# Three edits in an attention and mixture-of-experts kernel: the order of one PSUM copy and two exponentials, a weight decode in two parts, two constant casts moved

## The chip, the cores and the metric

One NeuronCore of a Trainium2 chip runs the whole program. The metric is device microseconds of one execution. Engines: TensorE (PE, with its weight loads PEld), VectorE (DVE), ScalarE (ACT), GpSimd (POOL), SyncE (SP), which here issues the DMAs.

## What is computed

Causal attention with a decay, on 4 x 8 heads of 576 tokens and width 64, then a dense gated layer, then a routed layer with 8 experts. Only the first part is touched by the change, apart from weights of the second that are prepared during it.

```python
scores = scale * np.matmul(q, k.transpose(0, 1, 3, 2))
decay = cum[:, :, :, None] - cum[:, :, None, :]
scores = np.where(causal, -1000000000.0, scores + decay)
scores = scores - np.max(scores, axis=-1, keepdims=True)
attn = np.exp(scores)
attn = attn / (np.sum(attn, axis=-1, keepdims=True) + 1e-09)
out = np.matmul(attn, v)
...
x = (silu(x @ w_gate) * (x @ w_val)) @ w_out
...
```

## The kernel before

Attention goes over 16 pairs of heads (`run`, L235). While pair p's probabilities are transposed and multiplied with the values, the scores of pair p+1 are made, so one turn of the loop holds both. The 576 queries are five tiles (0 to 4, tile 4 with all 576 keys).

`qk(p, i)` (L119) makes the scores of tile i for both heads: PE products into PSUM tiles `ps_s` (L144; tile 4 in two halves of 288 keys), DVE reductions that add the mask, take the row extreme and write the scores to SBUF (L151), and two ACT exponentials that sum their rows (L158). `tr(p, g)` (L161) transposes the probabilities in four groups, g = 0 to 3, into PSUM tiles `ps_t`, of which there are two; PE instructions are L170, L185, L187 and L180, the copies out of PSUM are ACT's L172 (group 0) and L193 (first head), and DVE's L191 (second head; both heads in group 3). The text calls group 2 the third and group 3 the fourth. Group 3's transposes write the two `ps_t` tiles that the copies of group 2 release. `av(p, g)` (L196, products L201) multiplies a group with the values. `rb` (L204) and `rt` (L210) make the reciprocals of the row sums, transpose them on PE (L214, once in a pair, just after group 0) and spread them by DMA (L219, L221). `xout` (L223) copies the result out of PSUM (L228 ACT, L229 DVE) and scales and splits it on POOL (L230, L232, L233).

In turn p, PE's order is that of the program: group 0, L214, scores of tiles 2 and 3; group 1, `av` 0, tile 4; group 2, `av` 1, tiles 1 and 0; group 3, `av` 2, `av` 3. PE alone is in written order (`manual_schedule`). The other engines' queues are put in order by a planner that takes the traced order as priority and simulates when each instruction becomes ready; `with issue_after(x)` adds an edge so that what the block traces on x's engine is queued behind x.

`run` calls two hooks of `tile_kernel`: `early` (L891) at the start of a turn, `late` (L899) after group 1's copies. At p = 1, `early` calls `cst.rest()` (L861): the DMA of constants (L863) and two DVE casts (L864, L865) of `U` and `ones`, which only the routing after the dense layer uses. From p = 2, every even turn fetches one part of the dense layer's first weights (L304), and every odd turn (3 to 13) decodes it.

The decode (L307) turns 64-bit floats into fp32 pairs: ACT's Square (L314), three DVE integer instructions L315, L316, L317 that build the word from both halves, POOL's L320 and L321 (test for tiny values), L326 (high part) and L329 (low part). In `late` it is queued behind group 1's ACT and DVE copies:

```python
with tc.issue_after(at.mark[0].ins), tc.issue_after(at.mark[1].ins):
    m1.decode(*todo.pop(0), eng=nc.gpsimd)
```

`mark[0]` and `mark[1]` are the last ACT and DVE copies that `tr` traced.

Of the kernel before, what the change touches and what calls it, by code (L numbers as in the profile page):

```python
# [13 lines left out]
ACTF = mybir.ActivationFunctionType  # L14
# [25 lines left out]
class Attention:  # L40
# [64 lines left out]
    def load(self, p):  # L105
        nc = self.nc
        qk = self.R[p] = self.raw.tile([128, 2, S], F32, name="qk")
        nc.sync.dma_start(out=qk, in_=self.io["qk"][2 * p:2 * p + 2].rearrange("a d t s -> (a d) t s"))
# [7 lines left out]
        ins = self.nc.sync.dma_start(out=self.dk[p % 2][61:67], in_=self.cd[2 * p:2 * p + 2].rearrange("a r s -> (a r) s"))  # L116
        self.mark[2] = self.mark[2] or ins

    def qk(self, p, i):  # L119
        nc = self.nc  # L120
        r, d = self.R[p], self.dk[p % 2]
        q0, m = QT[i]
        w = q0 + m
        rs = self.rs[p % 2]
        if p not in self.E:
            self.E[p] = [self.ep.tile([128, 1536], F32, name="e") for _ in range(2)]
        es = ([self.e0[2 * (p % 2) + a] for a in range(2)] if i == 0 else
              [e[:, EO[i]:EO[i] + w] for e in self.E[p]])
        mask = self.cst["mask"]
        off = 448 + m - w if m == 128 else 512  # L130
        b = 128 - m
        prev = [None, None]
        for lo, hi in [(0, w)] if w <= 512 else [(0, w // 2), (w // 2, w)]:
            n = hi - lo
            ps = [self.ps_s.tile([128, 512], F32, name="ps_s") for _ in range(2)]
            for c in range(2):
                for a in range(2):
                    h = 64 * a
                    x, y = r[h:h + 64, 0, q0:w], r[h:h + 64, 1, lo:hi]
                    if c and p:  # L140
                        x, y = self.neg[h:h + 64, :m], d[h:h + 64, lo:hi]
                    elif c:
                        x, y = self.cst["sel"][h:h + 64, :m], self.c8[h:h + 64, lo:hi]
                    nc.tensor.matmul(ps[a][b:, :n], x, y, start=c == 0, stop=c == 1, tile_position=(h, b))  # L144
            for a in range(2):
                mx = self.sm.tile([128, 1], F32, name="mx")
                o, x, y = es[a][b:, lo:hi], ps[a][b:, :n], mask[b:, off + lo:off + hi]
                if i in (1, 2):
                    o, x, y = (t.rearrange("p (b k) -> p b k", k=64) for t in (o, x, y))
                    o = o[:, ::-1]  # L150
                nc.vector.tensor_tensor_reduce(  # L151
                    out=o, in0=x, in1=y, scale=-0.125,
                    scalar=BIGF if prev[a] is None else prev[a][b:], op0=ALU.add, op1=ALU.min, accum_out=mx[b:],
                )
                prev[a] = mx
        for a in range(2):
            c = a * 5 + i
            nc.scalar.activation(es[a][b:, :w], es[a][b:, :w], ACTF.Exp, bias=prev[a][b:], scale=-1.0,  # L158
                                 accum_out=rs[b:, c:c + 1])

    def tr(self, p, g):  # L161
        nc = self.nc
# [72 lines left out]
    def run(self, extra, pool):  # L235
        dec = self.decay_load(pool)
        self.load(0)
        self.cst.load()
        self.decay(*dec)
        self.vload(0)  # L240
        self.load(1)
        self.rows(1)
        with self.tc.issue_after(self.mark[2].ins):
            self.vload(1)
        with self.tc.manual_schedule(engines={PE}):
            self.warm(WARM0)
            for i in (2, 3, 4, 1, 0):
                self.qk(0, i)
            for p in range(NP):
                with self.tc.issue_after(self.mark[2].ins):  # L250
                    if p + 2 < NP:
                        self.load(p + 2)
                    extra[0](p)
                nx = p + 1 < NP
                self.rb(p)
                for g, qs in enumerate(((2, 3), (4,), (1, 0), ())):
                    self.tr(p, g)
                    if g == 0:
                        self.rt(p)
                    elif g == 1:  # L260
                        extra[1](p)
                    if 0 < g < 3:
                        self.av(p, g - 1)
                    if nx:
                        for i in qs:
                            self.qk(p + 1, i)
                for g in range(2, 4):
                    self.av(p, g)
                if p + 2 < NP:
                    self.rows(p + 2)  # L270
                    self.vload(p + 2)
                self.xout(p)
# [14 lines left out]
class MoE1:  # L287
# [19 lines left out]
    def decode(self, r, hi, lo, eng=None):  # L307
        nc = self.nc
        rv = r.rearrange("p (n t) -> p n t", t=2)
        hv, lv = rv[:, :, 1], rv[:, :, 0]  # L310
        t = self.tmp.tile([128, 512], I32, name="dt")
        s = self.tmp.tile([128, 512], F32, name="ds")
        hf = r.bitcast(F32).rearrange("p (n t) -> p n t", t=2)[:, :, 1]
        nc.scalar.activation(s, hf, ACTF.Square)  # L314
        nc.vector.tensor_scalar(t, hv, 0x07ffffff, 3, op0=ALU.bitwise_and, op1=ALU.logical_shift_left)  # L315
        nc.vector.scalar_tensor_tensor(t, hv, -0x40000000, t, op0=ALU.bitwise_and, op1=ALU.bitwise_or)  # L316
        nc.vector.scalar_tensor_tensor(t, lv, 29, t, op0=ALU.logical_shift_right, op1=ALU.bitwise_or)  # L317
        tf = t.bitcast(F32)
        if eng:
            eng.tensor_scalar(s, s, 2.0 ** -30, None, op0=ALU.is_ge)  # L320
            eng.tensor_mul(s, s, tf)  # L321
        else:
            nc.vector.scalar_tensor_tensor(s, s, 2.0 ** -30, tf, op0=ALU.is_ge, op1=ALU.mult)
        s3 = s.rearrange("p (a b) -> p a b", a=hi.shape[1])
        if eng:
            eng.tensor_copy(hi, s3)  # L326
        else:
            nc.scalar.activation(hi, s3, ACTF.Copy)  # L328
        nc.gpsimd.tensor_sub(lo, s3, hi.bitcast(F32))  # L329

    def load(self, g):
        for src, hi, lo in self.parts(g):
            self.decode(self.fetch(src), hi, lo)

    def parts(self, g):
        io = self.io
# [66 lines left out]
H0, WARM0 = 2, 10  # L403
# [435 lines left out]
class Consts(dict):  # L839
# [21 lines left out]
    def rest(self):  # L861
        nc = self.nc
        nc.sync.dma_start(out=self.t[:, 128:], in_=self.src[:, 128:NCST])  # L863
        nc.vector.tensor_copy(self["U"], self.uf[0])  # L864
        nc.vector.tensor_copy(self["ones"], self.uf[1])  # L865


def tile_kernel(tc, io, out, dbg=None):
    nc = tc.nc
    with ExitStack() as ctx:  # L870
# [4 lines left out]
        cst = Consts(nc, cp, io["cst"])  # L875
        wts = Weights(nc)
        wts.pools.append(pool(ctx, "wA", 6))
        with ExitStack() as c1:
# [5 lines left out]
            m1 = MoE1(tc, c1, cst, io, wts, raw, tmp, xth, xtl)  # L884
            with ExitStack() as ca:
                cst.attention(pool(ca, "acst"))
                at = Attention(tc, ca, cst, io, xth, xtl)

                todo = []

                def early(p):  # L891
                    if p == 1:
                        cst.rest()
                    if p == H0:
                        todo.extend(m1.parts(0))
                    if p >= H0 and (p - H0) % 2 == 0 and todo:
                        todo[0] = m1.fetch(todo[0][0]), *todo[0][1:]

                def late(p):  # L899
                    if p > H0 and (p - H0) % 2 and todo:  # L900
                        with tc.issue_after(at.mark[0].ins), tc.issue_after(at.mark[1].ins):
                            m1.decode(*todo.pop(0), eng=nc.gpsimd)

                at.run((early, late), wts.pools[0])
            m1.open(c1)
            wab = [wts.pools[0], pool(c1, "wB", 6)]
            slp = pool(c1, "slots", space=PSUM)
# [6 lines left out]
            for i in range(len(steps) + 1):  # L914
                for f in range(2):
                    if i < len(steps):
                        g, t0, n = steps[i]
# [104 lines left out]
```

## Time and profile before

| what | us |
|---|---|
| median of 3 runs | 1012.9 |
| lowest, highest | 1008.58, 1015.99 |
| the profiled execution, its own time | 1005.57 |
| its span, first to last instruction | 1003.8 |
| PE busy | 944.4 (94%) |
| DVE, ACT, POOL busy | 597.3, 411.9, 228.4 |

The rows below are from that one profiled execution; times in them count from the start of its span. A row of instructions in order of time has the start, the length, engine, line, operation, names, shapes, the number of instructions merged into it, and in brackets how long the engine was idle before it and what ended that.

### The profile page before, as it was taken

The page shows a single profiled execution, that of the slowest core. Times are in us where ns is not written, and L with a number is a line of the kernel's source. Part 1 is how long each engine was busy: PE and PEld are TensorE (multiplying, and loading weights), DVE is VectorE, ACT ScalarE, POOL GpSimd, SP SyncE. Part 2 cuts the span into 40 slices and gives each one's busy share as a digit, 9 for nine tenths or more (in the row PEclk, how much of TensorE's full clock was granted, in tenths as well). Part 3 has the DMA queues.
Part 4 walks back from the last instruction along what each step waited for, and adds up shares of the span by engine and source line. Part 5 has one row for each costly group of instructions (what it writes and reads, how often), then busy time and mean ns, then how long its engine had stood idle before and what let it go on. Part 6 is the DMA issues. An engine that isn't in the chain of part 4 may idle for free.

```text
span 1003.8 us, 16493 instructions
## 1 busy us (share of the span) xinstructions
PE 944.4 (94%) x6282; PEld 847.5 (84%) x6282; DVE 597.3 (60%) x1421; ACT 411.9 (41%) x903; POOL 228.4 (23%) x205
## 2 busy tenths in 40 slices
PE   8899999999999999999999999999899999699893
PEld 5555555579999999999999999998799999699692
DVE  6566776759457468468467455677865554343720
ACT  5556666644343132132132123333554555244620
POOL 1244444442021011011011000000244434631111
PEclk9999999999999999999999999999899999989997
DMA  5344444313122012012012000113576576750400
GB/s 165 102 130 114 143 134 136 107 43 105 43 64 63 1 53 74 1 47 81 1 42 64 1 1 22 43 58 133 185 226 185 183 229 184 231 174 27 132 30 25
DMA packets 53088, 94.83 MB, mean 94 GB/s; under 512 B 5954, under 2 KB 27086, under 8 KB 53007
## 3 DMA queue, kind: packets, MB, share of 16 engines
q1 hardware_dynamic: 47503, 79.58, 26.0%
q0 software_dynamic: 5504, 14.17, 4.2%
q8 instruction: 50, 0.82, 0.3%
q14 instruction: 31, 0.25, 0.1%
HBM read 84.10 MB, written 10.16 MB: 94 GB/s over the span
## 4 chain that ended last, share of the span: by engine, by line
PE 57%; issue 16%; DVE 12%; POOL 6%; ACT 3%; DMA 3%; POOLq 0%; SPq 0%; DVEq 0%; ACTq 0%
PE ps_g L365 23%; PE ps_y L383 12%; PE ps_s L144 4%; DVE dt L316 3%; PE avy L201 3%; PE ps_t L185 3%; PE m_psg L659 3%; PE m_psy L674 2%; PE avx L201 2%; POOL out L700 2%; DVE dt L317 1%; ACT e L158 1%; POOL w L329 1%; DVE e L151 1%; DVE dt L315 1%
## 5 line engine op out<-in xcount | busy, mean ns | idle before, releaser
L365 PE MATMUL ps_g<-xth,w 128*128 128x384 f32 (+1 forms) x1184 | 308.6, 331 | 0.0
L365 PEld LDWEIGHTS ps_g<-xth,w 128*128 128x128 f32 x1184 | 213.1, 188 | 0.6
L365 PE MATMUL ps_g<-xtl,w 128*128 128x384 f32 (+1 forms) x592 | 196.1, 331 | 0.0
L383 PE MATMUL ps_y<-hh,w 128*128 128x384 f32 (+1 forms) x592 | 161.2, 333 | 2.9 <-DVE y L389 2.2
L659 PE MATMUL m_psg<-ygh,w 128*128 128x304 f32 x512 | 117.4, 311 | 1.2 <-ACT b_o L809 0.8
L674 PE MATMUL m_psy<-h2h,w 128*128 128x304 f32 x512 | 114.6, 306 | 0.5 <-issue 0.5
L383 PEld LDWEIGHTS ps_y<-hh,w 128*128 128x128 f32 x592 | 107.1, 188 | 5.8 <-DVE y L389 4.0
L329 POOL TENSOR_TENSOR w<-ds,w 128x512 fp32r<-128x512 f32 x36 | 49.8, 1384 | 271.9 <-ACT w L328 271.4
L365 PEld LDWEIGHTS ps_g<-xtl,w 128*128 128x128 f32 x592 | 111.2, 188 | 0.1
L158 ACT ACTIVATE e<-e,mx 128x320 f32<-128x320 f32 (+4 forms) x160 | 88.5, 555 | 51.7 <-DVE mx L151 51.2
L586 DVE TENSOR_TENSOR w<-raw,w 128x1024 fp32r<-128x1024 f32 x64 | 76.8, 1222 | 37.9 <-ACT w L585 22.4
L383 PE MATMUL ps_y<-hl,w 128*128 128x384 f32 (+1 forms) x296 | 97.9, 331 | 0.5 <-DVE hl L373 0.5
L372 ACT ACTIVATE hh<-hs 128x384 fp32r<-128x384 f32 (+1 forms) x74 | 38.2, 517 | 134.4 <-DVE hs L371 134.4
L370 DVE SCALAR_TENSOR_TENSOR hs<-hs,ps_g 128x384 f32<-128x384 f32 (+1 forms) x74 | 40.0, 541 | 86.4 <-ACT hs L369 86.4
L659 PEld LDWEIGHTS m_psg<-ygh,w 128*128 128x128 f32 x512 | 87.4, 193 | 1.8 <-ACT b_o L809 0.9
L674 PEld LDWEIGHTS m_psy<-h2h,w 128*128 128x128 f32 x512 | 85.5, 188 | 0.3
L151 DVE CUSTOM_DVE_ANT_0 e<-ps_s,mask 128x320 f32<-128x320 f32 (+4 forms) x160 | 62.6, 429 | 37.5 <-PE ps_s L144 36.6
L585 ACT ACTIVATE w<-raw 128x1024 fp32r<-128x1024 f32 x64 | 67.5, 1059 | 34.1 <-PE m_psg L659 13.3
L659 PE MATMUL m_psg<-ygl,w 128*128 128x304 f32 x256 | 78.4, 306 | 0.5 <-DVE ygl L627 0.5
L389 DVE TENSOR_TENSOR y<-ps_y,y 128x384 f32<-128x384 f32 (+1 forms) x124 | 67.2, 542 | 19.0 <-PE ps_y L383 18.2
L369 ACT ACTIVATE hs<-ps_g 128x384 f32<-128x384 f32 (+1 forms) x74 | 35.4, 479 | 104.6 <-PE ps_g L365 104.5
L674 PE MATMUL m_psy<-h2l,w 128*128 128x304 f32 x256 | 77.4, 302 | 0.0
(305 smaller groups left out, 1520.0 us busy)
## 6 DMA issues: line engine op xcount, KB each, us to landing
raw<-w SPq DMA_DIRECT2D x64, 512.0 KB
qk<-qk SPq DMA_DIRECT2D x16, 576.0 KB
v<-vL SPq DMA_DIRECT2D x16, 448.0 KB
raw<-mg SPq DMA_DIRECT2D x12, 512.0 KB
raw<-mv SPq DMA_DIRECT2D x12, 512.0 KB
raw<-mo SPq DMA_DIRECT2D x12, 512.0 KB
rb<-rd SPq DMA_DIRECT2D x16, 288.0 KB
yd<-yr SPq DMA_DIRECT2D x18, 256.0 KB
```

The costliest lines, as they stand in the source:

```text
L144: nc.tensor.matmul(ps[a][b:, :n], x, y, start=c == 0, stop=c == 1, tile_position=(h, b))
L151: nc.vector.tensor_tensor_reduce(out=o, in0=x, in1=y, scale=-0.125, scalar=BIGF if prev[a] is None else prev[a][b:], op0=ALU.add, op1=ALU. ...
L158: nc.scalar.activation(es[a][b:, :w], es[a][b:, :w], ACTF.Exp, bias=prev[a][b:], scale=-1.0, accum_out=rs[b:, c:c + 1])
L201: nc.tensor.matmul(self.X[x][64 * a:64 * a + 64, d0:d0 + n], v[k0:k0 + k, a, j], self.T[g, a][k0:k0 + k, o:o + n], start=g == 0, stop=g == ...
L329: nc.gpsimd.tensor_sub(lo, s3, hi.bitcast(F32))
L365: nc.tensor.matmul(ps[:, :n], w[:, k, fs], x[:, k], start=(k == 0 and c == 0), stop=(k == 3 and c == 2))
L383: nc.tensor.matmul(ps[:, :n], w[:, f, ds], h[:, f, :n], start=(f == 0 and c == 0), stop=(f == 1 and c == 2))
L389: nc.vector.tensor_add(y, ps[:, :n], y)
L585: nc.scalar.activation(hi, r, ACTF.Copy)
L586: nc.vector.tensor_sub(lo, r, hi.bitcast(F32))
L659: nc.tensor.matmul(ps[:, :C], w[:, k, fs], x[:, k], start=(k == 0 and c == 0), stop=(k == 3 and c == 2))
L674: nc.tensor.matmul(self.P[e][d][:, :C], w[:, f, ds], h[:, f], start=(u == 0 and f == 0 and c == 0), stop=(u == 3 and f == 1 and c == 2))
```

## The change

Tile 4's two exponentials are no longer traced with its scores but returned as a function, and traced in the next group's step behind group 2's ACT copy (`issue_after(mark[0])`). `decode` becomes a generator with one `yield`: Square and L315 stay in `late`, the rest (L316, L317 and the POOL instructions) is traced in a third hook, `last`, after group 2's copies and queued behind them on ACT and DVE; no edge is added on POOL. The two casts of constants move from turn 1's start to a function `split`, traced in `last` of turn 2; the DMA of the constants stays. Elsewhere the decode runs through both parts at once, as before.

```diff
-    def qk(self, p, i):
+    def qk(self, p, i, later=False):
...
-        for a in range(2):
-            c = a * 5 + i
-            nc.scalar.activation(es[a][b:, :w], es[a][b:, :w], ACTF.Exp, bias=prev[a][b:], scale=-1.0,
-                                 accum_out=rs[b:, c:c + 1])
+        def exps():
+            for a in range(2):
+                c = a * 5 + i
+                nc.scalar.activation(es[a][b:, :w], es[a][b:, :w], ACTF.Exp, bias=prev[a][b:], scale=-1.0,
+                                     accum_out=rs[b:, c:c + 1])
+
+        if later:
+            return exps
+        exps()
...
+                exps = None
                 for g, qs in enumerate(((2, 3), (4,), (1, 0), ())):
                     self.tr(p, g)
                     if g == 0:
                         self.rt(p)
-                    elif g == 1:
-                        extra[1](p)
+                    elif g < 3:
+                        extra[g](p)
+                    if exps:
+                        with self.tc.issue_after(self.mark[0].ins):
+                            exps()
+                        exps = None
                     if 0 < g < 3:
                         self.av(p, g - 1)
                     if nx:
                         for i in qs:
-                            self.qk(p + 1, i)
+                            exps = self.qk(p + 1, i, i == 4)
...
         nc.vector.tensor_scalar(t, hv, 0x07ffffff, 3, op0=ALU.bitwise_and, op1=ALU.logical_shift_left)
+        yield
         nc.vector.scalar_tensor_tensor(t, hv, -0x40000000, t, op0=ALU.bitwise_and, op1=ALU.bitwise_or)
...
         nc.sync.dma_start(out=self.t[:, 128:], in_=self.src[:, 128:NCST])
+
+    def split(self):
+        nc = self.nc
         nc.vector.tensor_copy(self["U"], self.uf[0])
         nc.vector.tensor_copy(self["ones"], self.uf[1])
...
+                dec = []
+
                 def late(p):
                     if p > H0 and (p - H0) % 2 and todo:
+                        dec.append(m1.decode(*todo.pop(0), eng=nc.gpsimd))
                         with tc.issue_after(at.mark[0].ins), tc.issue_after(at.mark[1].ins):
-                            m1.decode(*todo.pop(0), eng=nc.gpsimd)
-
-                at.run((early, late), wts.pools[0])
+                            next(dec[0])
+
+                def last(p):
+                    with tc.issue_after(at.mark[0].ins), tc.issue_after(at.mark[1].ins):
+                        if p == H0:
+                            cst.split()
+                        if dec:
+                            for _ in dec.pop():
+                                pass
+
+                at.run((early, late, last), wts.pools[0])
```

## Rows read from the trace of the kernel before

**Rows 1.** Busy time by stage: start:end, us, each engine's busy us, granted clock, DMA

```profile
0.00:218.00 218.00, 199.69 (x1618) 125.19 (x1619) 145.88 (x530) 135.08 (x409) 84.84 (x85) 0.96 0.42 123
218.00:700.00 482.00, 478.52 (x2832) 467.49 (x2832) 304.78 (x640) 145.23 (x285) 46.13 (x33) 1.00 0.15 46
```

**Rows 2.** Windows: pair 0; decode pairs 11, 13, all six; eight others

```profile
17.14:35.21 18.07, 14.49 (x99) 8.80 (x100) 8.01 (x33) 7.69 (x25) 0.17 (x1) 0.81 0.23 64
...
159.84:174.82 14.98, 13.27 (x101) 8.27 (x100) 10.58 (x34) 8.51 (x27) 8.95 (x8) 0.89 0.56 162
186.33:199.94 13.61, 11.89 (x100) 7.35 (x100) 10.60 (x34) 8.51 (x27) 8.66 (x7) 1.00 0.36 103
sum 84.90, PE 74.90 PEld 46.31 DVE 62.63 ACT 50.95 POOL 51.42; mean PE 12.48 PEld 7.72 DVE 10.44 ACT 8.49 POOL 8.57
...
sum 91.29, PE 91.29 PEld 56.70 DVE 61.33 ACT 64.46 POOL 27.17; mean PE 11.41 PEld 7.09 DVE 7.67 ACT 8.06 POOL 3.40
```

**Rows 3.** Who waited for whom, 0 to 222 us: total, times, longest

```profile
PE ps_t L180 <- ACT ath L193: 7.8, 6, 1.4
```

**Rows 4.** In order of time, pair 11 (L214 at 159.84), with a decode

```profile
163.65 0.42 DVE L315 TENSOR_SCALAR dt<-raw 128x512 int32<-128x512 int32 x1
163.74 1.62 POOL L233 TENSOR_TENSOR xtl<-xt,xth 128x576 fp32r<-128x576 f32 x1
...
164.10 1.80 DVE L316 SCALAR_TENSOR_TENSOR dt<-raw,dt 128x512 int32<-128x512 int32 x1
...
165.44 1.82 POOL L320 TENSOR_SCALAR ds<-ds 128x512 f32<-128x512 f32 x1
...
165.94 0.98 DVE L317 SCALAR_TENSOR_TENSOR dt<-raw,dt 128x512 int32<-128x512 int32 x1
...
166.84 0.45 DVE L151 CUSTOM_DVE_ANT_0 e<-ps_s,mask 128x288 f32<-128x288 f32 x1
...
170.31 0.33 PE L180 MATMUL ps_t<-cst,e 64*128 64x64 f32 x2 [1.35 <-ACT ath L193]
```

**Rows 5.** In order of time, pair 14 (L214 at 199.94), no decode

```profile
205.37 0.27 PE L187 MATMUL ps_t<-cst,e 128*128 128x128 f32 x1
...
205.80 0.78 ACT L158 ACTIVATE e<-e,mx 128x576 f32<-128x576 f32 x1 [1.09 <-DVE mx L151]
...
206.12 0.69 DVE L191 COPY ath<-ps_t 128x512 f32<-128x512 f32 x1
...
207.34 0.58 ACT L193 ACTIVATE ath<-ps_t 128x512 f32<-128x512 f32 x1
...
207.85 0.36 DVE L151 CUSTOM_DVE_ANT_0 e<-ps_s,mask 128x192 f32<-128x192 f32 x1 [1.03 <-PE ps_s L144]
207.96 0.20 PEld L180 LDWEIGHTS ps_t<-cst,e 64*128 64x128 f32 x2
...
208.25 0.46 ACT L158 ACTIVATE e<-e,mx 128x192 f32<-128x192 f32 x1 [0.33 <-DVE mx L151]
...
208.95 0.89 DVE L191 COPY ath<-ps_t 128x320 f32<-128x320 f32 x2
...
209.09 1.45 PE L201 MATMUL avy<-ath,v 128*64 128x256 f32 x12
```

**Rows 6.** In order of time, pair 0 (L214 at 17.14)

```profile
29.63 0.23 DVE L864 CAST uo<-cst 128x128 fp32r<-128x128 f32 x1 [4.60 <-DMA cst<-cst]
...
29.90 0.69 DVE L191 COPY ath<-ps_t 128x512 f32<-128x512 f32 x1
...
30.64 0.27 PE L180 MATMUL ps_t<-cst,e 64*128 64x64 f32 x1 [3.58 <-DVE ath L191]
...
31.71 2.35 PE L201 MATMUL avy<-ath,v 128*64 128x256 f32 x12
```

**Rows 7.** The decode's DVE lines in 0 to 222 us: ns least, median, most

```profile
L315 DVE TENSOR_SCALAR dt<-raw x6: 418/526/1620, 61.7 to 190.1; 128x512 int32<-128x512 int32 x6
...
L316 DVE SCALAR_TENSOR_TENSOR dt<-raw,dt x6: 693/1448/1797, 62.3 to 191.7; 128x512 int32<-128x512 int32 x6
```

More of the change, by code (lines that the diff above doesn't have):

```diff
@@ L332, in load @@
         for src, hi, lo in self.parts(g):
-            self.decode(self.fetch(src), hi, lo)
+            for _ in self.decode(self.fetch(src), hi, lo):
+                pass
     def parts(self, g):
@@ L897, in early @@
                         todo[0] = m1.fetch(todo[0][0]), *todo[0][1:]
+                dec = []
                 def late(p):
                     if p > H0 and (p - H0) % 2 and todo:
+                        dec.append(m1.decode(*todo.pop(0), eng=nc.gpsimd))
                         with tc.issue_after(at.mark[0].ins), tc.issue_after(at.mark[1].ins):
-                            m1.decode(*todo.pop(0), eng=nc.gpsimd)
-                at.run((early, late), wts.pools[0])
+                            next(dec[0])
[5 more added lines that the diff above has]
+                            for _ in dec.pop():
+                                pass
+                at.run((early, late, last), wts.pools[0])
             m1.open(c1)
```

## The prediction

> **What bounds the kernel now.** I read the busy times by stage first, then pair by pair, then who waits for whom, then single pairs in order of time. TensorE (PE) sets the end. From 218 to 700 us it is busy 478.52 of 482.00 us, so whatever the first stage gives up is passed on to the end almost whole [rows 1]. The attention stage before it is different: 199.69 busy of 218.00. I cut that stage at the transpose of the reciprocals (L214), which comes once in each pair of heads. The eight pairs that carry no decode take 91.29 us together, PE busy all of it: 11.41 us a pair is PE's own work, and nothing there can be won without taking work from PE. The six pairs with a decode (3, 5, 7, 9, 11, 13) take 84.90 us, 16.4 more than six of the others. Pair 0 takes 18.07 [rows 2].
>
> Two things make up the excess of a decode pair. One is PE's idle time: in six of them the first transpose of the fourth group (L180) waits for ACT's copy L193, 7.8 us in all [rows 3]. The other is the clock. In pair 11, one of three such, the granted clock is 0.89 of full speed on average, so PE was for a while at 1.2 and not at 2.4 GHz, and it is busy 13.27 us with the work that takes 11.41 elsewhere: 1.9 us a pair. Pair 13 kept 1.00 and took 13.61 [rows 2].
>
> Pair 11 shows the chain [rows 4]. The decode's three DVE instructions stand ahead of the reductions of tile 4. L315 takes 0.42, L316 1.80, L317 0.98. Tile 4's reductions begin only when they are through, at 166.84. After the reductions come two exponentials, then the ACT copy, and PE gets its PSUM buffer at 170.31 after 1.35 idle. In pair 14 that copy also stands behind the exponentials (207.34), but it ends at 207.92 and PE takes L180 at 207.96 without a recorded wait [rows 5].
>
> In pair 0 DVE waits 4.60 us for the constants' DMA with the cast L864; the third group's copy L191 stands behind it and starts at 29.90, and PE's second transpose of the fourth group has stood idle 3.58 when it starts at 30.64. The 12 products that follow take 2.35 us [rows 6] against 1.45 in pair 14 [rows 5].
>
> **The change, part by part.** *Constants.* The two casts leave pair 0's stretch and follow the third group's copies of pair 2. Their transfer, landed by 29.6, is then long done. In pair 2 DVE is idle there for 1.03 us (pair 14 stands for it [rows 5]), and 0.23 [rows 6] for each cast hides under that: cost 0; without the cover it is 0.3. What goes in pair 0 is 3.6 of idle and 2.35 - 1.45 = 0.9 of slow clock: 4.5 us. Late next there would be the loads of pair 1 and 2, which are issued where they were; the DMA of the constants stays in SP's place too. Nothing moves past another transfer on SP's queue: the edit moves the casts and leaves the issue.
>
> *Copy before exponentials.* In pair 14 the last transpose for the copy ends at 205.64 and the exponentials of tile 4 begin at 205.80, after ACT has been idle for 1.09 [rows 5]. The copy (0.58) then runs at about 205.7 to 206.3, the exponentials start some 0.5 later and, at 0.78 a step, end at about 207.95, before the first exponential of tile 1 (208.25). Cost 0 there; if that slack of 0.3 were gone, it is up to 0.58 a pair. Behind the copy on ACT wait the two exponentials, and behind them those of tiles 1 and 0; these feed the next pair's reciprocals. In a decode pair the copy no longer waits for reductions that the decode has delayed: the idle 1.35 before L180 goes.
>
> *Decode in two places.* The Square and L315 stay; L316, L317 and the POOL steps move behind the third group's copies. No instruction or DMA is added. I follow a decode pair from its L214 on. DVE's third-group copy ends at +6.8 as in pair 14 (206.81 - 199.94, less the overlap of about 0.1 with which DVE starts the next). L316 and L317 at 0.69 [rows 7] and 0.69 (a twin of it, bounded by 0.98 [rows 4]) run to +8.2. Tiles 1 and 0 began at +7.9 (207.85); they now start 0.3 to 0.6 late, take the 1.1 that they take to the next copy (208.95), and the two copies of the fourth group (0.89) end at +10.2 to +10.5 instead of +9.9. The last products need them: the 12 products that contain them start at +9.15, and the third of them that reads these copies is due two thirds of 1.45 later, at about +10.1 to +10.3. So PE loses 0 to 0.35; I take 11.6 us for the pair. That holds where L315 takes 0.42.
>
> L315 can take 1.62 [rows 7]. In pair 11 it started 0.09 before POOL's L233, and got through at 0.42; L316 started 0.36 behind it and took 1.80 [rows 4]. The least L316 took is 0.69 [rows 7]. L315 stays where it is, next to L233, so I count three slow and three fast. Slow is 1.2 later, of which the fourth group's copies, ending at about +11.1, pass 0.7 on beyond the fast case: 12.3 us. Half of each gives 3 x 11.6 + 3 x 12.3 = 71.7, a gain of 84.9 - 71.7 = 13.2.
>
> The bounds: below, six pairs at 11.41, a gain of 16.4. Above, L316 and L317 at 1.80 and 0.98 in the new place too (1.4 more) on top of the slow L315: 13.7 a pair, a gain of 2.7. I stay near the first, because in the new place POOL has ended L233 (165.36, that is +5.5) and has only L320, begun at +5.6, before it must wait for L317.
>
> The Trainium skill (SBUF — State Buffer, section "Who interferes with whom") says that VectorE and GpSimd share one pair of SBUF ports, and that a GpSimd instruction and a VectorE one with two SBUF inputs, or in a two-port mode, exclude each other for a whole instruction, the later one blocking fully. The trace agrees for L316 (1.80 beside L233, 0.69 at the least). Held strictly, the rule speaks against the new place: L320, recorded from +5.6 for 1.82 us, would hold L316 until +7.4, 0.6 late in each of six pairs, and the sum would come out 3.6 us poorer than mine. It is the first rival's mildest form.
>
> **The sum.** 13.2 + 4.5 = 17.7 us. The profiled execution took 1005.57 us (span 1003.8 and 1.8 around it): 987.9 on its own terms. The runs shown have a median of 1012.9, 7.3 above that execution; taking the same gain from it gives 995.2.
>
> **Rivals.** *POOL holds the second part as well.* POOL's L320 is the next in its queue after L233, and if it holds L316 and L317 as L233 did (1.80 and 0.98), a fast pair becomes 11.6 + 1.4 = 13.0: gain 84.9 - 78.0 + 4.5 = 11.4, 1001.5 us. For: L317 at 0.98 behind L320's start. Against: POOL's next step (L321) must wait for L317, so only one instruction can be in the way.
>
> *Another wait in pair 0.* If PE, 4.5 us earlier at pair 1, meets a load that isn't there, pair 0's part is lost: 13.2 alone, 999.7. Against: the queries and keys were issued ahead of the constants, whose transfer had landed at 29.6.
>
> *The exponentials bind.* They come 0.58 later in all 15 pairs; if the slack of 0.3 on ACT is spent (an ACT copy that waits for PE), the reciprocals of the next pair come late by up to 0.58: 15 x 0.58 = 8.7 given back, gain 9.0, 1003.9.
>
> *Slower.* The lateness moves to the end of the pair: all three decode steps are held by POOL, the fourth group's copies come after av2 is through, PE idles there and the clock falls to 1.2 GHz, which pair 11 prices at 1.9. Then a pair takes 12.3 + 1.4 + 1.9 = 15.6, six 93.6: 8.7 more than before, less 4.5 from pair 0, 1017.1. It decides against the change from 14.9 us a pair on (14.15 now, plus 4.5 / 6).
>
> *The change doesn't do what it says.* DVE and ACT follow an order that a planner makes; if it puts the pieces where the waits stay, the time stays 1012.9. Against: the edges that the change adds are binding for that order.
>
> **How the numbers follow.** Forecast 0.66, POOL 0.13, pair 0 0.08, exponentials 0.07, slower 0.03, nothing 0.03. A measurement of this kernel tells about 1% from no change, 10 us: below 1002.8 is faster. The forecast nearly whole, six tenths of POOL's case, most of pair 0's case and a third of the exponentials' make 0.82; slower by over 1% needs more than the worst rival, 0.02; 0.16 between. The range: 1005 above, which holds the bound of 2.7 + 4.5 = 7.2 but for a fraction and leaves out the last two rivals. Below, all six at 11.41 gives 16.4 + 4.5 = 20.9, 992.0; and if the runs shown lost the clock in the three other decode pairs too (3 x 1.9 of the 7.3 that they lie above the profiled one), the gain grows to 26.6: 986.3, so I say 985.
>
> **What would show it.** Right: decode pairs at 11.4 to 12.5 us with a granted clock of 1.00; L316 at about 0.7; no wait of L180 for L193; ACT's copy ahead of tile 4's exponentials; pair 0 at about 13.5 us; the casts without idle time. Wrong: a new wait of the last products (L201) for DVE's L191 of over 1 us, L316 near 1.8, a clock of 0.89 in a decode pair, or pairs without decode above 11.6.

## The result and the profile after

The changed kernel's first set of runs has a median of 995.81 us (990.16 to 1006.24, 5 runs) beside 1009.75 (1008.32 to 1015.99, 5 runs) for the kernel before on the same chip: ratio 0.9848 [0.9807, 0.9888]. The forecast was 995.2. Two further sets, taken with the experiments, gave 998.66 beside 1009.41, 0.9923 [0.9892, 0.9955], and 999.14 beside 1006.88, 0.992 [0.9899, 0.994]. So the change gains 7.7 to 13.9 us by medians, about 11. That is faster by over 1% in the first set and inside 1% in the others: the direction held, but the gain is smaller than the forecast 17.7 us. The changed kernel also scatters more (995.15 to 1006.97 in the second set) than the kernel before (1006.56 to 1013.17 there, in 12 runs).

The profile first taken of the changed kernel was its slowest run, so I read the one of the second set (995.15 us, span 993.3). L158 is L159 and L180 is L185 after the change, L191 is L196, L193 is L198, L201 is L206, L233 is L238, L315 is L325, L316 and L317 are L327 and L328, L320 is L331, and rd's and rb's DMAs, L219 and L221, are L224 and L226.

Stretches of the changed kernel: pairs 0, 7, 11, 12 and 14; then three stretches of pairs 12 and 13; the last is a stretch of routing, at the start of the routed experts. A row has the stretch, its length, the busy us of PE, PEld, DVE, ACT and POOL, the clock as a share of 2.4 GHz, the DMA share and GB/s. They answer to [rows 1, 2].

```profile
17.19:30.05 12.86, 12.86 (x99) 7.67 (x100) 7.66 (x31) 7.65 (x25) 0.00 (x0) 0.87 0.31 90
99.76:112.84 13.08, 11.70 (x100) 7.05 (x100) 11.11 (x34) 8.57 (x27) 7.45 (x6) 1.00 0.47 125
148.13:159.65 11.52, 11.52 (x100) 7.06 (x100) 9.19 (x34) 8.58 (x27) 3.08 (x3) 1.00 0.45 119
159.65:171.50 11.85, 11.44 (x102) 7.08 (x100) 8.53 (x31) 8.41 (x27) 7.03 (x7) 1.00 0.72 193
183.09:196.72 13.63, 11.52 (x102) 7.29 (x101) 7.67 (x31) 8.04 (x26) 9.30 (x8) 1.00 0.34 104
...
162.00:169.00 7.00, 7.00 (x69) 4.54 (x69) 5.25 (x23) 5.53 (x18) 2.88 (x3) 1.00 1.01 281
169.00:174.00 5.00, 4.59 (x37) 2.69 (x34) 3.42 (x10) 2.77 (x10) 3.46 (x3) 1.00 0.14 51
174.00:175.60 1.60, 1.60 (x18) 0.98 (x18) 1.60 (x6) 1.60 (x6) 0.00 (x0) 1.00 0.00 0
...
695.18:703.18 8.00, 7.40 (x35) 6.61 (x34) 5.48 (x31) 1.68 (x4) 4.16 (x5) 0.50 0.38 94
```

Pair 0 went from 18.07 [rows 2] to 12.86. Pair 11 went from 14.98 at a clock of 0.89 to 11.52 at 1.00. The six decode pairs sum to 72.97 us (11.65, 12.62, 13.08, 12.51, 11.52, 11.59), where they were 84.90. These are 5.2 and 11.9 us. But pair 14, which has no decode, takes 13.63 and loses 2.1 in one wait, and pair 12 takes 11.85; both had 11.5 before. The attention stage ends at 203.18 instead of 217.85 us, 14.7 earlier. The rest of the span took 790.1 instead of 785.9. Of these 4.2, 1.5 are lost in the dense layer (the first product of the routing, `rt_ps<-yh`, starts at 606.00 instead of 619.16) and 1.8 more at the start of the routed experts (their first product, `m_psg<-ygh`, at 703.68 instead of 715.05). The last row shows TensorE at 1.2 GHz there, where the kernel before had 0.93 of 2.4 GHz in the eight us at the same distance from its attention stage (the row stands further down).

PE's waits in the attention stage (total, times, longest), which answer to [rows 3]:

```profile
PE avy L206 <- DVE ath L196: 3.1, 3, 1.4
PE ps_s L144 <- DMA qk<-qk: 2.3, 2, 2.1
```

The wait of the transpose for ACT's copy, 7.8 us before, is gone from the list. Two others stand there in its place. The decode's three instructions (ns least, median, most), which answer to [rows 7]:

```profile
L325 DVE TENSOR_SCALAR dt<-raw x6: 417/417/424, 56.5 to 175.3; 128x512 int32<-128x512 int32 x6
...
L327 DVE SCALAR_TENSOR_TENSOR dt<-raw,dt x6: 682/920/1497, 59.5 to 178.3; 128x512 int32<-128x512 int32 x6
...
L328 DVE SCALAR_TENSOR_TENSOR dt<-raw,dt x6: 692/836/1778, 60.2 to 179.0; 128x512 int32<-128x512 int32 x6
```

In order of time, a pair that is slow and one that is fast (pair 7, begun at 99.76, and pair 11, begun at 148.13); [rows 4] show pair 11 of before:

```profile
105.01 1.42 POOL L235 TENSOR_TENSOR xt<-xt,rb 128x576 f32<-128x576 f32 x1 [9.59 <-DMA rb<-rd]
...
106.54 1.16 DVE L327 SCALAR_TENSOR_TENSOR dt<-raw,dt 128x512 int32<-128x512 int32 x1
...
107.23 1.73 POOL L238 TENSOR_TENSOR xtl<-xt,xth 128x576 fp32r<-128x576 f32 x1
...
107.74 1.78 DVE L328 SCALAR_TENSOR_TENSOR dt<-raw,dt 128x512 int32<-128x512 int32 x1
...
111.06 1.04 PE L206 MATMUL avy<-ath,v 128*64 128x256 f32 x4 [1.38 <-DVE ath L196]
...
153.93 0.60 ACT L198 ACTIVATE ath<-ps_t 128x512 f32<-128x512 f32 x1 [0.48 <-PE ps_t L192]
...
154.43 0.77 ACT L159 ACTIVATE e<-e,mx 128x576 f32<-128x576 f32 x1
...
154.92 0.68 DVE L327 SCALAR_TENSOR_TENSOR dt<-raw,dt 128x512 int32<-128x512 int32 x1
...
155.63 0.69 DVE L328 SCALAR_TENSOR_TENSOR dt<-raw,dt 128x512 int32<-128x512 int32 x1
...
156.12 0.33 PE L185 MATMUL ps_t<-cst,e 64*128 64x64 f32 x2
...
156.43 1.41 POOL L235 TENSOR_TENSOR xt<-xt,rb 128x576 f32<-128x576 f32 x1 [9.95 <-DVE dt L328]
```

The reader is to see three things. ACT's copy now stands ahead of tile 4's exponentials and L185 waits for nothing. L325 is never held in this profile. And in pair 7 POOL's normalisation of the pair before (L235 to L238) starts 5.25 us after the pair's begin, because it has waited 9.59 us for the broadcast of the reciprocals, rb; it then runs beside L327 and L328, which take 1.16 and 1.78 instead of 0.68 and 0.69. The fourth group's copies end 1.4 us too late for the last products. Pairs 5, 7 and 9 lose so; in the profile of the third set it is pairs 5 to 11, at 12.65 to 12.84 us.

What delays rb is seen on SP's queue. First its waits in 60 to 200 us (total, times, longest), then DMA issues in order of time and PE's wait in pair 14, in the changed kernel:

```profile
SPq L226 <- DMA rd<-rt: 94.0, 12, 11.8
```
```profile
162.17 0.63 SPq L224 DMA_DIRECT2D rd<-rt  x1
174.62 0.51 SPq L226 DMA_DIRECT2D rb<-rd  x1
175.18 0.46 SPq L108 DMA_DIRECT2D qk<-qk  x1
...
185.47 0.81 PE L144 MATMUL ps_s<-qk 64*128 64x320 f32 x4 [2.11 <-DMA qk<-qk]
```

The kernel before: the same wait of SP (60 to 215 us), and four stretches.

```profile
SPq L221 <- DMA rd<-rt: 36.6, 13, 3.4
```
```profile
24.00:27.00 3.00, 3.00 (x29) 1.89 (x28) 1.03 (x6) 2.11 (x5) 0.00 (x0) 1.00 0.16 56
27.00:29.60 2.60, 0.06 (x1) 0.00 (x0) 0.00 (x0) 0.00 (x0) 0.00 (x0) 1.00 0.11 44
...
709.85:717.85 8.00, 6.74 (x47) 5.77 (x46) 6.59 (x28) 4.00 (x7) 4.47 (x5) 0.93 0.52 150
```

SP issues rd (the reciprocals, 5 KB, written to memory), waits until it has landed, and issues rb (their broadcast from there over 128 rows); the next pair's queries and keys stand behind rb in SP's order. From rd's issue to rb's it took 2.1 us in pair 1, 5.7 in pair 5, 10.2 in pair 11, and 12.5 in pair 12 (162.17 to 174.62); before, it was 1.2 to 3.8 in the 16 pairs. I call this the lag.

The three stretches from 162 on show why, with the packets that the trace records. The broadcast issued at 159.15 is 128 packets of 2304 bytes. They move from 160.43 to 168.46, 37 GB/s, never more than three at once, while the other loads beside them bring the share to 1.01. Then for 5 us the share is 0.14, that is 2.2 of 16 engines, and 51 GB/s. No packet of the broadcast is left by then: what moves are the last parts of the queries and keys, the weights and the values, which were issued behind it. rd, issued at 162.17, is ten packets of 512 bytes; eight move by 169, and the last two at 173.7, after those parts. Then nothing moves until rb's next issue. From one issue of rb to the next it takes 12.8 us on average (pair 1 to pair 13), in both kernels. Before, TensorE's own round was 12.6 ((84.90 + 91.29) / 14 [rows 2]), so the lag didn't grow. After, TensorE asks for 11.3 to 11.6, and the transfers don't follow. The Trainium skill (DMA: Bandwidth & Descriptors, section "Rules for kernel authors") says that a DMA whose outermost dimension has c under 16 steps, for example a leading broadcast of c copies, is confined to at most c engines; rb's source is [2, 64, S], and the trace agrees: never more than four packets of rb move at once in any pair, and 2.2 of 16 engines are left with work behind it.

### The profile page after: what moved, and what is told of

It reads as the page before. It is cut to its first block, busy times and chain, and to the rows that moved or that the text cites. A ratio compares the mean times of both kernels' runs of the same rounds, so it can differ in the third digit from the quotient of the medians.

```text
span 1004.4 us, 16481 instructions
## 1 busy us (share of the span) xinstructions
PE 943.2 (94%) x6282; PEld 845.8 (84%) x6282; DVE 597.1 (59%) x1421; ACT 412.3 (41%) x903; POOL 227.1 (23%) x205
## 4 chain that ended last, share of the span: by engine, by line
PE 56%; issue 16%; DVE 9%; DMA 8%; POOL 7%; ACT 3%; SPq 0%; another core or an unknown queue 0%; POOLq 0%; DVEq 0%; ACTq 0%
PE ps_g L377 23%; PE ps_y L395 12%; PE ps_s L144 5%; PE m_psy L686 3%; PE ps_t L190 3%; PE m_psg L671 3%; DMA rd<-rt 2%; DVE dt L327 2%; DMA qk<-qk 2%; PE avx L206 2%; PE avy L206 2%; POOL out L712 2%; POOL w L340 1%; DMA raw<-w 1%; POOL b_r L652 1%
## 5 line engine op out<-in xcount | busy, mean ns | idle before, releaser
L159 ACT ACTIVATE e<-e,mx 128x320 f32<-128x320 f32 (+4 forms) x160 | 88.0, 551 | 32.9 <-DVE mx L151 32.4
L686 PEld LDWEIGHTS m_psy<-h2h,w 128*128 128x128 f32 x512 | 86.7, 191 | 0.3
L597 ACT ACTIVATE w<-raw 128x1024 fp32r<-128x1024 f32 x64 | 67.4, 1058 | 40.1 <-PE m_psg L671 12.5
```

The source lines that it names most:

```text
L597: nc.scalar.activation(hi, r, ACTF.Copy)
L686: nc.tensor.matmul(self.P[e][d][:, :C], w[:, f, ds], h[:, f], start=(u == 0 and f == 0 and c == 0), stop=(u == 3 and f == 1 and c == 2))
```

## The experiments

**The three edits, each alone.** Two theories stood against each other: that each edit gives its own term of the sum, or that a transfer sets a floor that any of them reaches. "Copy alone" and "decode alone" have the casts back at their old place; in "copy alone" and "casts alone" the decode is in one piece (the first hunk); "casts alone" and "decode alone" have the exponentials in line (the second).

```diff
-                            next(dec[0])
+                            for _ in dec.pop():
+                                pass
```
```diff
-                            exps = self.qk(p + 1, i, i == 4)
+                            self.qk(p + 1, i)
```

The changed kernel again: 

> The changed kernel once more, for a second profile. Prediction's steps (P): 17.7 us less, ratio 0.982 to 0.983, decode pairs at 11.5 to 12.5 us to the last, no wait for a load. Rival (D), from the first profile after: the transfers have become the bound. There the reciprocals' broadcast (rb) moved at about 50 GB/s with a DMA share of 0.13 for some 5 us, and SP's round of a pair (rd, rb, qk, raw, dk, v) took about 13 us against 11.4 of TensorE, so that the wait between the issue of rd and that of rb grew from 2 us in pair 1 to 12.7 in pair 12. D expects the same growth here, TensorE waiting for queries and keys in pairs 12 to 14, the first decode pairs near 12 and pair 13 at 14 us or more, and a total gain of 13 to 15 us, ratio 0.985 to 0.987.

Measured 998.66, 0.9923 [0.9892, 0.9955]; its profile is the one above. The lag grew to 12.5 us as D had it. The gain is below both ranges, and it was pair 14 and not pair 13 that took over 13 us.

Copy alone: 

> Only the ACT copy ahead of tile 4's exponentials; decode in one piece, casts where they were. P: TensorE's idle before L180 (1.35 us in a decode pair) goes, the 0.35 before tile 1's scores stays, and the clock with less idle time stays up: decode pairs at 12.2 to 12.5, 74 us for six, 11 less: 0.989. Rival (V): VectorE's copy for the second head still stands behind the delayed reductions and takes ACT's place as the last to come, so L180's second transpose waits instead: decode pairs near 14, gain about 1: 0.999. D, in either case: no more than about 8 us, since SP's round is about 12.8 to 13 us a pair: 0.992.

Measured 1000.6, 0.9919 [0.9895, 0.9944]: the number that D gave, but not by D's floor, as its lag shows below.

Casts alone: 

> Only the two casts of constants moved. P: pair 0 takes 13.0 us in place of 18.1, nothing else changes: 4.5 to 5 us less, 0.995. D: the pairs after it already take 12.8 us on average, which is SP's round, so some of the 5 us is given back as waits for loads: 0.997 to 1.000.

Measured 1001.94, 0.992 [0.9892, 0.9947]: more than either theory gave it.

Decode alone: 

> Only the decode in two parts. P: tile 4's reductions are on time, so the ACT copy behind the exponentials is on time as in the pairs without decode, and this edit alone takes the decode pairs to about 12.0: 13 us less, 0.987; with the copy alone at 0.989 the two edits would not add. Rival: the copy behind the exponentials still makes L180 wait by about 0.5, pairs at 12.5: 0.990. D: as for the copy alone, 8 us at most: 0.992.

Measured 1002.71, 0.9927 [0.9902, 0.9952].

By the medians the single edits gain 8.8, 7.5 and 6.7 us, 23.0 together, and all three at once gain 10.8: they do not add. Some of the waits (total, times, longest) follow, for copy alone, decode alone and casts alone, in this order:

```profile
DVE uo L879 <- DMA cst<-cst: 6.4, 1, 6.4
...
PE ps_s L144 <- DVE mx L151: 3.9, 6, 1.0
```
```profile
DVE uo L879 <- DMA cst<-cst: 4.1, 1, 4.1
...
PE ps_s L144 <- DMA qk<-qk: 3.4, 3, 1.9
```
```profile
PE ps_t L185 <- ACT ath L198: 8.0, 6, 1.4
```

Each mechanism appears where the prediction had it: without the moved casts DVE waits 4.1 to 6.4 us for the constants; without copy and split, L185 waits 8.0 in six. With copy alone the whole decode still delays DVE's reductions, and the scores wait 3.9 us for them.

Copy and split overlap: with either one alone the wait of L185 for ACT's copy is gone. The six decode pairs take 77.6 us with copy alone, 74.1 with decode alone and 73.0 with all three, beside 84.9 before. The floor shows in decode alone: its decode pairs 3 to 11 take 11.88 to 12.29, it meets the queries and keys three times, as the changed kernel does in pair 14, and its lag goes to 12.2 us. In copy alone and casts alone the lag stays below 7 us and no such wait exceeds 0.2, so there the floor is not what they reach.

The profiles do not show where the sum of the medians goes. The attention stage ends 6.7 us earlier with copy alone, 2.1 with casts alone and 5.3 with decode alone, 14.1 together, and 14.7 with all three. In casts alone pair 0 gives 3.8, but the decode pairs take 86.7, three of them at a clock of 0.81 to 0.89; its profiled execution took 1006.29, 4.3 above its median. What the medians lack of 23.0 is open.

**The broadcast in two transfers.** If rb's two engines set the floor, two DMAs of 64 rows each must lift it, for the changed kernel and for the kernel before:

```diff
-        self.mark[2] = nc.sync.dma_start(out=rb, in_=d.unsqueeze(1).to_broadcast([2, 64, S]))
+        for a in range(2):
+            self.mark[2] = nc.sync.dma_start(out=rb[64 * a:64 * a + 64], in_=d[a:a + 1].to_broadcast([64, S]))
```

The change with it: 

> The changed kernel with the broadcast of the reciprocals (rb) issued as two transfers of 64 rows each in place of one of 2 x 64. D (the transfers bound the changed kernel, through rb, which moves at 50 GB/s with a DMA share of 0.13, as if on two of sixteen engines, and holds what is queued behind it): rb now takes under 2 us, the wait between rd's and rb's issue stays below 4 us to the last pair, no wait for queries and keys in pair 14 (2.1 us in the second profile), decode pairs 11.5 to 11.9, attention ends at 197 to 199 us in place of 203.2, and the time is 5 to 8 us below the changed kernel's: 0.975 to 0.986 of the kernel before. Rival (S): SP's order is the bound, since rb waits on its queue for rd's landing and everything of the next pair waits behind it, however wide rb is: lag grows to 10 us as it did, time as the changed kernel's.

Measured 972.75 beside 995.39 for the kernel before on the same chip: 0.9762 [0.9739, 0.9785].

The kernel before with it: 

> The kernel before with rb in two transfers and nothing else. If rb's late landing is what puts POOL's scaling and splitting (L230 to L233) beside the decode's VectorE steps, and what keeps the constants' transfer (9.4 us for 237 KB) behind it: POOL is done by 4 us into a pair, L315 and L316 take 0.42 and 0.70 in all six decode pairs, these take 12.2 us as pair 7 did (73 for six, 11 to 12 us less), and the cast's wait of 4.6 falls below 1: 4 more. 0.984 to 0.989. Rival: the POOL steps are held by something else (the order on POOL, ACT's copy), L316 stays at 1.8 in most pairs: 0.995 to 1.0.

Measured 977.65, 0.9819 [0.9797, 0.984]: somewhat more than expected.

In the change with the wide broadcast, pair 11, the stretch of pair 13 in which rb (issued at 173.50) is the only load that moves, and SP's wait in 60 to 200 us:

```profile
145.79:157.31 11.52, 11.52 (x100) 7.06 (x100) 9.20 (x34) 8.58 (x27) 8.00 (x7) 1.00 0.65 207
174.80:176.40 1.60, 1.60 (x16) 0.83 (x16) 1.57 (x5) 1.60 (x4) 0.80 (x1) 1.00 0.63 187
```
```profile
SPq L227 <- DMA rd<-rt: 27.5, 12, 3.6
```

The 288 KB move in 1.6 us at a share of 0.63, 187 GB/s. All decode pairs take 11.5 to 11.7, PE never waits in them, the lag is at most 3.9 us, and the attention stage ends at 198.2. The floor was the broadcast's. A second rival, that SP's own order binds whatever the width, fell with it. The ratio is 0.016 below the changed kernel's, about 16 us and not the 5 to 8 expected. The attention stage gives 5.0 of them, and the dense layer, in which this kernel loses nothing, another 1.5; the rest is not located, and the chips differ.

The other kernel says more. With this one edit and nothing of the change, the attention stage ends at 202.6, as early as the whole change has it. Its views, in this order: the two stretches of pair 0 that stand above for the kernel before; PE's wait; the decode's second instruction; and POOL and DVE in pair 11, begun at 148.84.

```profile
24.00:27.00 3.00, 3.00 (x30) 2.05 (x28) 2.25 (x12) 1.28 (x4) 0.00 (x0) 1.00 0.30 117
27.00:29.60 2.60, 2.60 (x30) 1.65 (x28) 1.77 (x10) 2.26 (x9) 0.00 (x0) 1.00 0.01 3
```
```profile
PE ps_t L180 <- ACT ath L193: 6.1, 6, 1.0
```
```profile
L317 DVE SCALAR_TENSOR_TENSOR dt<-raw,dt x6: 692/694/694, 58.6 to 176.7; 128x512 int32<-128x512 int32 x6
```
```profile
148.93 1.40 POOL L231 TENSOR_TENSOR xt<-xt,rb 128x576 f32<-128x576 f32 x1 [7.79 <-ACT xt L229]
150.39 0.66 POOL L233 CAST xth<-xt 128x576 fp32r<-128x576 f32 x1
151.13 1.42 POOL L234 TENSOR_TENSOR xtl<-xt,xth 128x576 fp32r<-128x576 f32 x1
...
152.66 0.42 DVE L316 TENSOR_SCALAR dt<-raw 128x512 int32<-128x512 int32 x1
153.11 0.69 DVE L317 SCALAR_TENSOR_TENSOR dt<-raw,dt 128x512 int32<-128x512 int32 x1
153.84 0.69 DVE L318 SCALAR_TENSOR_TENSOR dt<-raw,dt 128x512 int32<-128x512 int32 x1
```

(Its lines are one or two beyond those of before.) In pair 0 of the kernel before, the constants landed late because their transfer stood behind the two-engine broadcast: shares of 0.16 and 0.11 from 24 to 29.6, PE idle in the second stretch. With two DMAs they are there by 26.6 and the casts wait for nothing; the pair takes 14.03, at a clock of 0.79. In a decode pair POOL has rb when the pair's sums are ready, and is through at 152.55, 0.11 before the decode's first DVE instruction. So all three run alone, at 0.42, 0.69 and 0.69, and so they do in all six pairs. A decode pair takes 12.2; the 1.0 that is left is L180's wait for ACT's copy, which the copy ahead of the exponentials removes.

**One edit taken out, with and without the wide broadcast.** Is the split of the decode still worth anything when the copy comes first? Copy and casts with the wide broadcast, the decode in one piece: 

> The changed kernel with rb in two transfers, but with the decode in one piece. If POOL is out of the way, one piece costs 1.8 us of VectorE ahead of tile 4's reductions, with the copy first PE loses under 0.7 us a decode pair: 12.0 each, 2 to 4 us slower than with the split. Rival (the split is what matters): pairs of 12.8 to 13 as in the run with the copy alone, 6 to 8 us slower.

Measured 970.99, 0.9759 [0.9737, 0.9781]: neither expectation, it is as fast as with the split.

Casts and split, no early copy, wide broadcast: 

> The changed kernel with rb in two transfers, but with tile 4's exponentials ahead of the copy as before. P: with the decode split the reductions are on time and the copy behind the exponentials makes no wait, so this equals the version with the copy first, within 2 us. Rival: the copy ahead of the exponentials is worth its 0.5 us in each pair: 3 to 7 us slower than with it.

Measured 979.05, 0.9828 [0.9803, 0.9853], 6.3 us slower than with the copy first: the rival's range. Its profile shows a granted clock of 0.95 in every pair after the first, so its stages can't be compared with the others', and it was measured again in the last set: 

> Again the changed kernel with rb in two transfers and the exponentials ahead of the copy. Its first profile had a granted clock of 0.95 throughout, and pairs without decode of 11.6 us. If that was the run's and not the version's: 11.4 for those, 11.9 for the decode pairs (VectorE's order has a reduction between L327 and L328 there), 0.979, some 3 us slower than with the copy first. If it is the version's: 0.95 and 0.983 again.

Measured 991.18, 0.9849 [0.9813, 0.9884], with pairs without decode back at 11.39 us (11.6 in the run before): the 0.95 was of that run, not of the edit. The ratio is again that of the rival all the same. The attention stage ends at 199.3, 1.1 later than with the copy first, so most of the 6 us lies outside it and is not located.

In the same set, the changed kernel: 

> The changed kernel beside the two below on one chip. D: 10 to 16 us less than the kernel before (0.984 to 0.990); the wait between rd's and rb's issue grows past 9 us again and TensorE waits for queries and keys in one of pairs 12 to 14.

Measured 999.14, 0.992 [0.9899, 0.994]: less than expected. The lag grew to 11.9 us, and TensorE waited 0.5 us for queries and keys.

The decode in one piece, rb as it was: 

> Copy first and casts moved, decode in one piece, rb in one transfer as in the changed kernel. P (terms add): 11 for the copy and 5 for the casts less, 16 us, so the split is worth 2 to 3 us of the forecast: 0.984. D: the transfers' round bounds it as it bounds the changed kernel, and the split is worth nothing: within 0.3% of the changed kernel.

Measured 992.7, 0.9861 [0.9838, 0.9884], its four runs within 0.9 us: between the two expectations.

The decode in one piece, wide broadcast: 

> The same with rb in two transfers, the fastest so far, beside the changed kernel: D: decode pairs 11.3 us as all others, 0.976 of the kernel before again, 9 to 15 us below the changed kernel.

Measured 985.75, 0.9788 [0.9756, 0.9819].

With the wide broadcast the split is worth nothing that these runs can tell: 0.9759 without it and 0.9762 with it. Its decode pairs take 11.32 without the split and 11.52 with it (the first 11.66 in both); with the split but no early copy they take 11.87 to 12.03, where PE waits 0.2 a pair for the fourth group's copies:

```profile
PE avy L206 <- DVE ath L196: 1.3, 6, 0.3
```

With rb as it was, the kernel without the split is measured faster than the changed kernel (992.7 and 999.14, intervals apart), though POOL then holds the one-piece decode at its old place. Its decode instructions, and its worst pair:

```profile
L325 DVE TENSOR_SCALAR dt<-raw x6: 417/1099/1536, 55.4 to 179.7; 128x512 int32<-128x512 int32 x6
...
L327 DVE SCALAR_TENSOR_TENSOR dt<-raw,dt x6: 693/1032/1034, 56.0 to 180.2; 128x512 int32<-128x512 int32 x6
...
L328 DVE SCALAR_TENSOR_TENSOR dt<-raw,dt x6: 692/1776/1786, 57.1 to 180.9; 128x512 int32<-128x512 int32 x6
```
```profile
100.66:115.88 15.22, 13.66 (x100) 8.29 (x100) 11.78 (x34) 8.60 (x27) 8.85 (x7) 0.89 0.46 130
```

Its attention stage ends at 205.1 us, 2.6 later than that of the changed kernel in the same set (202.5), whose profiled execution took 990.6, 8.5 below its median. So why the medians stand the other way round is not shown by these profiles. What differs is the lag, 11.9 us in the changed kernel and 8.0 without the split, and with it the dense layer, in which the first loses 1.7 us against the kernel before and the second 0.8.

The best version is the decode in one piece, copy first, casts moved, and the broadcast in two DMAs: 0.9759 and 0.9788 in its two sets, ahead of both kernels. Its interval overlaps that of the version with the split.

## Why the prediction was right, and where it wasn't

*Constants, 4.5 us.* Right: pair 0 gave 5.2, the casts stand in pair 2 without idle time (pair 2 takes 11.32, as pair 1, so no load was late there either). The 3.6 of idle went in every version with the casts moved. The other part, the clock, is not the edit's to give: these versions took 11.32 us in pair 0 at a clock of 1.00 up to 14.25 at 0.78 (casts alone), so the size was partly luck.

*Copy first, cost 0, and the idle 1.35 goes.* Right. The wait went from 7.8 us to none, though the split alone removes it too, and pairs that carry no decode stay at 11.3 to 11.4 but for 12 and 14. The rival in which the exponentials bind fell: it asked 0.58 in each of 15 pairs.

*Decode pairs, 71.7 us.* Measured 72.97, close for a partly wrong reason. The step "I count three slow and three fast" put the slow case on L315 staying beside L233. L325 took 0.42 in all six, so the slow case of 12.3, with its +11.1 that no row gives, was not met. It was the second part that was held, in pairs 5, 7 and 9, which took 12.62, 13.08 and 12.51. This is the rival in which POOL holds the second part, near its price of 13.0, in three of six; the other three took 11.5 to 11.65, the forecast's 11.6. The argument against it, that POOL has ended L233 by then and only L320 can be in the way, took POOL's times of before as given, while they hang on when rb lands, and rb moves later from pair to pair. What ran beside L327 and L328 in these pairs was mostly the normalisation, L235 to L238, which ends with the old L233. L320 (L331) did not hold L327 in pair 3: L327 took 0.68 from 59.48 on, while L331 is recorded from 58.30 to 59.80. In pairs 11 and 13 POOL comes so late that it falls behind the decode altogether (L235 at 156.43). The Trainium skill (SBUF — State Buffer, section "Who interferes with whom") says that a DVE instruction with two SBUF inputs contends with a GpSimd instruction that reads SBUF, and the trace agrees for L235 to L238: L327 takes 0.68 alone and up to 1.50 beside them, L328 0.69 and up to 1.78.

*What is late next.* This step failed. It named the loads of pairs 1 and 2, and said that nothing moves past another transfer on SP's queue. That is so for the order of issue, but nothing asked how long one round of that queue takes. The next limit was rd, rb and the queries and keys behind them, 12.8 us a round against TensorE's 11.4. The lag needs ten pairs to grow, so it costs TensorE a load only in pair 14, where it loses 2.2 us, 2.1 of them in the wait for queries and keys. Pair 12 loses 0.4 by another road: POOL scales so late that DVE's addition ahead of the reciprocals (L212) runs beside it and takes 1.14 us instead of 0.17, and L219 waits for that. The rows read before had the sign: pair 0 and the decode pairs were long in part for one common cause, since the wide broadcast alone removes the constants' wait, the slow decode instructions and the low clock of the decode pairs. It leaves 6.1 of the 7.8 us of L180's wait and a clock of 0.79 in pair 0. Two of the prediction's own signs of being wrong came: the last products wait up to 1.4 us for DVE's copy, and pairs 12 and 14 are above 11.6.

*Passed on to the end almost whole.* This failed too: where the prediction counted 17.7, the attention stage gave up 14.7 in the profile (17.1 in the terms that the sum held, 5.2 + 11.9, less about 2.6 for pairs 12 and 14), and 10.5 of these reached the end. The row it rested on ends at 700 us and shows TensorE busy; what lies behind 700 had no row. The dense layer lost 1.5 and 1.7 us in the two profiles of the changed kernel read here and 1.9 in decode alone, while in the six with the wide broadcast it is within 0.3 of the kernel before. So this loss goes with the broadcast; by which load is not shown. The routed experts are another matter: one profile of the changed kernel loses 2.7 us there, the other gains 1.3, so the change does not explain it.

*The median.* The first set's 995.81 lies on the forecast, partly by luck: the forecast started from 1012.9, the median of three runs, and with two more of the kernel before the start is 1009.75, so the gain was 13.9 and not 17.7. The second and the third set, 0.9923 and 0.992, lie above it, and a gain of 17.7 from 1009.41 would be 0.9825, outside both intervals. So the sum was some 7 us too hopeful by the medians of all sets. In the profile the two steps just named hold nearly all of it; what the other executions lose, and where, no profile isolates.

## What to carry to other kernels

When several waits of a stage look unrelated (a load that comes late, an engine that is held by another, a clock that falls), look for one slow transfer ahead of all of them before reordering instructions. Here a stretch of up to 5 us with a DMA share of 0.11 to 0.16 and work waiting was its mark: the loads behind it finishing on its few engines. Before counting the gain of a faster stage, take the length of each repeating round that runs beside it, the DMA queue's too, from issue to issue; a round that was just short enough becomes the next bound, and its lag may need many iterations to reach the bottleneck. Try each edit of a bundle alone: here three edits that gain 7 to 9 us each by the medians give about 11 together, and the split is worth nothing beside the others once the broadcast is wide.

## What the runs showed of the hardware that was not expected

A broadcast of 288 KB whose outermost dimension has 2 steps took 6.0 to 8.0 us in the changed kernel, 37 to 49 GB/s, with at most four packets moving at once. As two DMAs of 64 rows the same bytes took 1.6 to 3.1 us in the change with the wide broadcast, up to 181 GB/s, with up to 19 at once. It delayed what was issued behind it: with the broadcast already through, loads moved at 51 GB/s on 0.14 of the engines for 5 us. rd, of 5 KB, landed up to 11.8 us after SP began to wait for it, because its last two packets of ten stood behind those loads.

The decode's three DVE instructions on 128x512 took 0.42 to 1.62, 0.69 to 1.80 and 0.69 to 0.98 us in the kernel before, and 0.42, 0.69 and 0.69 in all six pairs with the broadcast in two: no change to DVE's own order, only to when a DMA let POOL start.
